# Attention units of two chunks of one batch, two tokens side by side on a partition, and more sums by accumulating DMA

## Chip, cores and metric

One core of a Trainium2 chip. The metric is the device time of one execution in microseconds (us). Each kernel was run beside the kernel before on the same chip, and fast runs are compared with fast runs; a run over 1.5% above the fastest of its kernel doesn't count as fast. A ratio is the mean time of one kernel's fast runs over that of the other's of the same rounds, so it is not quite the ratio of the medians that are quoted.

The engines: PE multiplies matrices (PEld are its weight loads), DVE is VectorE, ACT is ScalarE, POOL is GpSimd, SP is SyncE. In a line of a profile, L303 is line 303 of that kernel.

## The reference

Gated linear attention, token by token, followed by a two-layer block with a rational function in its middle. 4 batches, 8 heads, 768 tokens, head size 48; model width 384, inner width 2048.

```python
f = 1.0 / (1.0 + np.exp(-f_logit))
for t in range(S):
    state = f[:, :, t, :, None] * state + einsum('bhd,bhde->...', k[:, :, t], v[:, :, t])   # outer product k v^T
    y[:, :, t] = einsum('bhd,bhde->bhe', q[:, :, t], state)
x = y as (3072 tokens, 384)
h = x @ w_in
P = a[0] + a[1]*h + a[2]*h**2 + a[3]*h**3
Q = 1.0 + abs(b[0])*abs(h) + abs(b[1])*h**2
out = (P / (Q + 1e-6)) @ w_out
```

(The outer product is written in short here.) A kernel does this by chunks of 128 tokens: what a token gets from earlier chunks goes through the state (`q` times state), and what it gets from its own chunk goes through a masked matrix of scores (`scm`) times `v`. Both are summed into `y`.

## The kernel before

The work is cut into 12 units of 256 tokens. Before the change, a unit is one chunk of 128 tokens of two batches (`j` is the batch). All instructions of all units stand in one fixed list of steps (`STEPS`), which was tuned by hand. A unit has steps for the cumulative sums of the gates (`cs`), transposes (`tp`), scores (`sc`) and the update of the state (`sv`), a step `y`, then `xe` (its copy to `xT`), then two groups of the wide part: `hp = w_in . xT`, its copy, squares and sums, logarithm and exponential, and `op = gall . w_out`.

Loads take one DMA for each tensor and batch, in rows of one head of one token (48 x 4 B = 192 B):

```python
def rows(eng, dst, src, n):
    c, u = units[n]
    for j in range(UB):                                    # UB = 2
        eng.dma_start(out=dst[:, j],
                      in_=src[u * UB + j, :, c * C:(c + 1) * C, :].rearrange("h t d -> t h d"))
```

A head takes 48 columns, so it is put together from pieces of at most 32 output rows (`quad`). `r` says which 32 of the 128 output rows, and so which 32 columns of the PE array, a matmul uses.

```python
def mm(j, p, i, quad, lhsT, rhs):
    lo, hi = cols[p % 2, quad]
    qd = 3 * (p // 2) + quad
    r = 64 * i + 32 * (qd % 2)
    nc.tensor.matmul(y[r:r + hi - lo, qd // 2, j, :], lhsT[:, lo:hi], rhs,
                     start=False, stop=True, skip_group_check=True)

todo = [(j, p, i, quad) for j in range(UB) for half, quad in cols
        for p in range(half, HP, 2) for i in range(2)]
if s["c"] > 0:
    for j, p, i, quad in todo:                             # 32 matmuls of 48 rows x 32 columns
        r = slice(64 * i, 64 * i + D)
        mm(j, p, i, quad, s["st"][r, j, p, :], s["qkT"][r, j, 0, p, :])
for j, p, i, quad in todo:                                 # 32 matmuls of 128 rows x 32 columns
    mm(j, p, i, quad, s["vn"][:, j, p + HP * i, :], s["scm", j][:, i * HP + p, :])
```

So the number of rows used changes once inside a unit. Two sums of the rational function are done in one of several ways, chosen group by group of 24 groups: by DVE, by an accumulating DMA, or (`u` only) by PE through the identity.

```python
P_BY_DMA = {5, 7, 8, 10, 11, 13, 14, 15, 16, 17, 18, 19, 20, 21, 22}
U_BY_DMA = {3, 7, 8, 9, 10, 12, 13, 14, 17, 19, 21, 23}

def m_p(n):
    s = mg[n]
    if n in P_BY_DMA:
        nc.gpsimd.dma_start(out=s["t"], in_=s["pb"], accum_op=ALU.add)
    else:
        nc.vector.tensor_add(s["t"], s["t"], s["pb"])
```

## Time and profile before

| | kernel before |
|---|---|
| time, median (2 runs) | 254.75 us (253.52 to 255.97) |
| busy PE / DVE / ACT, of a span of 252.3 us | 207.8 / 213.6 / 207.6 us |
| all `y` phases together, first clearing to last start | 13.0 us |
| PE at half clock | 27.3 us, all in the first 81.5 us |

The page of the kernel before gives busy times of the engines, and the clock granted to PE in 40 slices of the span (9 is full):

```profile
PE 207.8 (82%) x2423; PEld 142.1 (56%) x2423; DVE 213.6 (85%) x238; ACT 207.6 (82%) x203; POOL 60.4 (24%) x77
...
PEclk9977959795897999999999999999999999999999
```

Three engines are nearly equally full, none above 85%, and the clock is full once the start is over.

### The profile page before, as it was taken

Reading aid. Unit: us, or ns where it says so; the run is one execution under the profiler, and the core shown is the slowest. Engines: PE = TensorE matmul, PEld = TensorE weight load, DVE = VectorE, ACT = ScalarE, POOL = GpSimd, SP = SyncE. Lnnn points to the kernel's source line nnn. Section 1 sums busy time; section 2 is a strip of 40 time slices with the busy share of each in tenths; the row PEclk is TensorE's granted clock in tenths of the full one; section 3 lists DMA queues with packets and bytes.
Section 4 is the critical chain, followed back from the end, with each engine's and each line's share of the span. In section 5 each row is a group of like instructions: output and inputs, shape, how many; then the busy total and the mean of one; then the engine's idle time right before and its main releaser. Section 6 shows DMA issues by size and latency. Waiting matters only on the chain.

```text
span 252.3 us, 5762 instructions
## 1 busy us (share of the span) xinstructions
PE 207.8 (82%) x2423; PEld 142.1 (56%) x2423; DVE 213.6 (85%) x238; ACT 207.6 (82%) x203; POOL 60.4 (24%) x77
## 2 busy tenths in 40 slices
PE   8667366946988898887998969989999999997754
PEld 2234254835664666565766746866576676574432
DVE  7122168899999999999999999979999999999940
ACT  2425427799899999998996999998999899999841
POOL 8046019000510200412223142124115022041100
PEclk9977959795897999999999999999999999999999
DMA  7999989999999996898999999489458859529921
GB/s 122 171 205 166 174 162 109 194 175 195 188 154 177 175 197 128 169 194 100 199 225 197 188 182 196 106 168 166 85 118 181 63 113 188 129 56 214 226 78 62
DMA packets 111338, 39.70 MB, mean 157 GB/s; under 512 B 101201, under 2 KB 107089, under 8 KB 111313
## 3 DMA queue, kind: packets, MB, share of 16 engines
q0 software_dynamic: 31792, 18.88, 54.3%
q1 hardware_dynamic: 79232, 20.45, 43.9%
q8 instruction: 19, 0.31, 0.6%
q14 instruction: 7, 0.05, 0.1%
q10 hardware_dynamic: 288, 0.00, 0.1%
HBM read 25.17 MB, written 4.72 MB: 118 GB/s over the span
## 4 chain that ended last, share of the span: by engine, by line
DVE 27%; DMA 25%; PE 14%; ACT 13%; issue 10%; SPq 9%; POOL 1%; DVEq 0%; POOLq 0%; ACTq 0%
DMA z<-h 9%; DMA t<-pb 8%; SPq L163 7%; PE hp L322 6%; DVE gall L407 5%; DMA qn<-in_q_dram 4%; DVE h L341 4%; PE op L424 4%; ACT y L336 4%; DVE scm L260 4%; DVE qkp L197 3%; DMA fn<-in_f_logit_dram 3%; ACT qi L377 3%; ACT lq L372 2%; DVE t L387 2%
## 5 line engine op out<-in xcount | busy, mean ns | idle before, releaser
L322 PE MATMUL hp<-xT,w_in_sb 128*128 128x256 bf16 x576 | 71.9, 280 | 3.7 <-ACT xT L309 2.1
L424 PE MATMUL op<-w_out_sb,gall 128*128 128x384 bf16 x368 | 67.1, 331 | 6.5 <-ACT osb L212 4.2
L322 PEld LDWEIGHTS <-w_in_sb 128*128 128x128 bf16 x576 | 56.9, 100 | 16.1 <-issue 5.8
L424 PEld LDWEIGHTS <-gall 128*128 128x128 bf16 x384 | 36.3, 98 | 31.3 <-issue 5.9
L336 ACT CAST y<-hp 128x1024 bf16<-128x1024 f32 x48 | 48.3, 1017 | 5.5 <-PE hp L322 4.9
L377 ACT ACTIVATE qi<-lq 128x2048 bf16<-128x2048 f32 x24 | 46.2, 1925 | 0.1
L372 ACT ACTIVATE lq<-z,sig 128x2048 f32<-128x2048 bf16 x18 | 36.2, 2011 | 5.1 <-DMA z<-h 5.0
L260 DVE TENSOR_TENSOR scm<-sc,mask 128x1024 bf16<-128x1024 f32 x24 | 29.1, 1214 | 6.5 <-PE sc L251 6.5
L341 DVE TENSOR_TENSOR h<-y 128x2048 bf16<-128x2048 bf16 x24 | 29.1, 1214 | 1.7 <-DMA z<-h 1.7
L364 POOL DMA_DIRECT2D z<-h x12 | 12.1, 1005 | 76.4 <-ACT A L190 25.4
L407 DVE TENSOR_TENSOR gall<-t,qi 128x2048 bf16<-128x2048 bf16 x24 | 29.0, 1215 | 1.5 <-DMA t<-pb 1.5
L396 POOL DMA_DIRECT2D t<-pb x15 | 14.8, 990 | 61.0 <-DVE t L387 56.1
L387 DVE TENSOR_TENSOR t<-t,h 128x2048 bf16<-128x2048 bf16 x24 | 28.9, 1215 | 0.0
L163 POOL DMA_DIRECT2D vpd<-in_v_dram x24 | 24.8, 1139 | 13.6 <-PE cs L182 13.5
L212 ACT COPY qkT<-tp 128x2048 bf16<-128x2048 bf16 x8 | 15.1, 1884 | 11.6 <-PE tp L206 11.6
L206 PE MATMUL tp<-ident,qkp 128*128 128x128 bf16 x192 | 14.5, 235 | 10.7 <-DVE qkp L197 10.0
L390 DVE TENSOR_SCALAR pb<-y,a_sb 128x2048 bf16<-128x2048 bf16 x24 | 19.3, 805 | 1.8 <-ACT y L336 1.0
L206 PEld LDWEIGHTS <-qkp 128*128 128x128 bf16 x192 | 12.9, 106 | 13.1 <-DVE qkp L197 12.0
L382 DVE TENSOR_SCALAR t<-y,a_sb 128x2048 bf16<-128x2048 bf16 x24 | 19.8, 825 | 0.1
L190 ACT ACTIVATE A<-cs 128x768 f32<-128x768 f32 x24 | 18.5, 818 | 0.6 <-PE cs L182 0.6
L197 DVE TENSOR_TENSOR qkp<-qn,A 128x768 bf16<-128x768 f32 x12 | 11.4, 950 | 8.5 <-DMA qn<-in_q_dram 8.5
L197 DVE TENSOR_TENSOR qkp<-kn,A 128x768 bf16<-128x768 f32 x12 | 11.4, 950 | 7.8 <-DMA kn<-in_k_dram 4.9
(63 smaller groups left out, 232.3 us busy)
## 6 DMA issues: line engine op xcount, KB each, us to landing
t<-pb POOLq DMA_DIRECT2D x15, 512.0 KB, 6.1
z<-h POOLq DMA_DIRECT2D x12, 512.0 KB, 6.1
fn<-in_f_logit_dram SPq DMA_DIRECT2D x24, 192.0 KB, 4.7
kn<-in_k_dram SPq DMA_DIRECT2D x24, 192.0 KB, 5.5
qn<-in_q_dram SPq DMA_DIRECT2D x24, 192.0 KB, 5.8
out_dram<-osb SPq DMA_DIRECT2D x24, 192.0 KB, 3.4
vpd<-in_v_dram POOLq DMA_DIRECT2D x24, 96.0 KB, 7.3
wst<-in_moe_w_in_dram SPq DMA_DIRECT2D x4, 384.0 KB, 8.5
```

The costliest lines, as they stand in the source:

```text
L163: eng.dma_start(out=dst[:, j], in_=src[u * UB + j, :, c * C:(c + 1) * C, :].rearrange("h t d -> t h d"))
L197: nc.vector.tensor_mul(paired(s["qk"][:, i]), s[("qn", "kn")[i]].rearrange(nat, i=2), s["A", i].rearrange(nat, i=2))
L206: nc.tensor.transpose(tp[:, j, i, p, :], s["qk"][:, i, p, j].rearrange("t i d -> t (i d)"), ident)
L260: nc.vector.tensor_mul(m, s["sc", j].rearrange("s i p t -> s (i p) t"), mb)
L322: nc.tensor.matmul(hp[:, e, :], w_in_sb[:, kk, f * P:(f + 1) * P], xT[:, kk, :], start=(kk == 0), stop=(kk == KD - 1))
L336: nc.scalar.copy(part_of(tile_of(n, "y"), half), mg[n]["hp", half].rearrange("p a n -> p (a n)"))
L341: nc.vector.tensor_mul(s["h2"], s["y"], s["y"])
L372: nc.scalar.activation(lq if whole else part_of(lq, half), s["u"] if whole else s["u", half].rearrange("p a n -> p (a n)"), AF.Ln, scale=s ...
L377: nc.scalar.activation(part_of(tile_of(n, "qi"), part, parts), part_of(mg[n]["lq"], part, parts), AF.Exp, scale=-1.0)
L387: nc.vector.tensor_mul(s["t"], s["t"], s["h2"])
L407: nc.vector.tensor_mul(galls[m][:, lo:lo + w, :].rearrange("p a n -> p (a n)"), part_of(s["t"], part, parts), part_of(s["qi"], part, parts))
L424: nc.tensor.matmul(ops[m, b], galls[m][:, mm, b * C:(b + 1) * C], w_out_sb[:, mm, :], start=(mm == 0), stop=(mm == KF - 1))
```

## The change

Its intent, as the diff reads: a unit becomes two successive chunks of one batch, with tokens 2p and 2p+1 side by side on partition p. A row of a load is then two tokens of one head, 384 B, and a load needs one DMA instead of two. Nine more sums become accumulating transfers (27 to 36), which relieves PE and DVE. The start is reordered, and the list of steps was made anew.

The core of the diff (the list of steps, the masks, the cumulative sums, the state update and the start are cut):

```diff
-P_BY_DMA = {5, 7, 8, 10, 11, 13, 14, 15, 16, 17, 18, 19, 20, 21, 22}
+P_BY_DMA = {4, 5, 6, 7, 9, 10, 11, 12, 13, 14, 15, 16, 17, 18, 19, 20, 21, 22}
-U_BY_DMA = {3, 7, 8, 9, 10, 12, 13, 14, 17, 19, 21, 23}
+U_BY_DMA = {2, 3, 4, 5, 6, 7, 8, 9, 11, 13, 15, 16, 17, 18, 19, 20, 21, 22}
...
+    def rows(src, n):
         c, u = units[n]
-        for j in range(UB):
-            eng.dma_start(out=dst[:, j],
-                          in_=src[u * UB + j, :, c * C:(c + 1) * C, :].rearrange("h t d -> t h d"))
+        return src[u, :, c * UB * C:(c + 1) * UB * C, :].rearrange("h (p b) d -> p h (b d)", b=UB)
...
-        cols = {(1, 1): (0, 32), (0, 0): (ZC, ZC + 32), (1, 2): (32, 64), (0, 1): (ZC + 32, 64)}
-
-        def mm(j, p, i, quad, lhsT, rhs):
+        cols = {(1, 1): (-16, 16), (0, 0): (0, 32), (1, 2): (16, 48), (0, 1): (32, 48)}
+
+        def head(p, i, quad):
             lo, hi = cols[p % 2, quad]
             qd = 3 * (p // 2) + quad
...
+            r = slice(64 * i + 32 * (qd % 2), 64 * i + 32 * (qd % 2) + hi - lo)
+            k_ = slice(64 * i, 64 * i + D)
+            for cc in range(UB):                           # the two chunks of the unit
+                w = slice(CH * cc, CH * cc + CH)
+                o = y[r, qd // 2, :, w]
+                if s["c"] + cc > 0:
+                    nc.tensor.matmul(o, s["st"][cc][k_, p * D + lo:p * D + hi], qcols(s, k_, p, w), ...)
+                for b in range(UB):                        # the two tokens of a partition
+                    v0 = (((p + HP * i) * UB + cc) * UB + b) * D
+                    nc.tensor.matmul(o, vf[:, v0 + lo:v0 + hi],
+                                     s["scm", p // 2][:, i, p % 2, b, :]..., ...)
...
+        for odd, quad in cols:
+            for p in range(odd, HP, 2):
+                for i in range(2):
+                    head(p, i, quad)
+            if (odd, quad) == (1, 1):
+                (clear the 16 rows that the pieces at -16 and at 16 have filled with a neighbour's columns)
```

`v` of a unit lies in `vz`, where each chunk fills 64 of 128 partitions and the rest stays zero, so `scm` matmuls keep 128 rows. The order inside `head` is: state (48 rows), `scm`, `scm` (128 rows), and the same for the second chunk. A unit has 96 matmuls for 64, and the number of rows changes 64 times instead of twice, counting the step from the clearing into the first state matmul. (The four first units have no state for their first chunk: 80 matmuls and 32 changes.)

## The prediction

> **What bounds the kernel now.** I read the table by windows first, because a mean over the span mixes three stages. This is the kernel before, cut at 80 and 230 us; the columns after the length are the busy time of PE, PEld, DVE, ACT and POOL, then granted clock, DMA share and GB/s.
>
> ```profile
> 0.00:80.00 80.00, 55.52 (x577) 36.74 (x578) 54.13 (x67) 52.09 (x52) 23.77 (x39) 0.84 1.26 168
> 80.00:230.00 150.00, 138.64 (x1767) 97.78 (x1766) 147.36 (x160) 143.19 (x142) 34.83 (x36) 0.99 0.90 155
> 230.00:252.00 22.00, 13.65 (x80) 7.62 (x79) 12.15 (x13) 12.26 (x11) 1.84 (x2) 1.00 0.59 139
> ```
>
> From 80 to 230 us three engines are nearly full at once: DVE 98% (147.36/150), ACT 95%, PE 92%. DVE ends this stage, but whatever adds more than some 11 us to PE there passes it. In the first 80 us nothing is full except the DMA engines; PE runs on 0.84 of its clock. The chain that ended last says the same of the start: it goes through the DMA queue's issues and through loads.
>
> ```profile
> 13.06 5.91 SPq L163
> 19.02 1.00 SPq L163
> 20.07 1.68 SPq L163
> 21.79 11.02 DMA qn<-in_q_dram
> 32.90 0.97 DVE qkp L197
> ```
>
> So until 33 us unit 1 waits for its q. That is what the wider rows aim at. The third view is PE's own order of time around one attention output `y`, late in the kernel at full clock, and the same early at half clock (start, length, instruction, count):
>
> ```profile
> 180.73 0.19 PE L268 MATMUL y<-zeros 128*128 128x1 bf16 x2
> 180.85 0.63 PE L277 MATMUL y<-qkT,state 48*32 48x128 bf16 x32
> 181.41 0.63 PE L277 MATMUL y<-scm,vpd 128*32 128x128 bf16 x32
> 181.97 1.47 PE L424 MATMUL op<-w_out_sb,gall 128*128 128x384 bf16 x8
> ```
>
> ```profile
> 58.02 1.04 PE L277 MATMUL y<-qkT,state 48*32 48x128 bf16 x32
> 59.00 1.05 PE L277 MATMUL y<-scm,vpd 128*32 128x128 bf16 x32
> ```
>
> One such matmul takes 216 to 219 ns alone, so at 180 us 32 of them start within 0.63 - 0.216 = 0.41 us. The single records show how: four start 3 to 4 ns apart (their results go to four different groups of 32 output rows), and the next four start 56 ns after the first of them. A matmul of 128 columns thus occupies its 32 columns of the array for 56 ns, and four run side by side. From the last state matmul to the first scm matmul (48 rows to 128 rows) it is 146 ns, in 9 of 9 cases after 80 us: 90 more than 56. The same surcharge stands wherever the shape changes: full-width hp to the 48-row sc takes 205 ns where hp to hp takes 109, sc to full-width hp 149 where sc occupies 56. At half clock the state to scm step took 241 ns, a group of four about 107.
>
> **What the Trainium skill says.** (1) TensorEngine Tiling (Array Packing), Tiling Modes, Key Properties: "Changing tiling mode (not just tile) drains the TensorE", and different tiles can run in parallel. The trace agrees on both: 90 to 97 ns for a change, four matmuls per 56 ns. (2) TensorE: Matmul & The Clock Gate, Part 1: the clock goes to half by how busy PE was in windows of about 3.4 us. The trace agrees: its clock records change in multiples of 3413 ns, 27.3 of the first 81.5 us lie at half clock, and none from there to 252 us, where PE is dense. What counts as busy the page does not settle here; see the rivals. (3) DMA: Bandwidth & Descriptors, Why small descriptors are slow: a fixed overhead per packet and descriptor. The DMA records agree: packets of 192 B took 19.1 ns on average, of 1536 B 71.7 ns, so eight times the bytes for 3.8 times the time.
>
> **The change part by part.** Twelve units remain, each of 256 tokens, but of one batch.
>
> Loads: 73,728 packets of 192 B become 36,864 of 384 B. Between the two points above, 384 B come to 19.1 + 192 x (71.7 - 19.1)/1344 = 26.6 ns (estimate). That is 1405 us of engine time down to 981; v (24,576 packets at 29.0 ns, now half as many at perhaps 33) 713 down to 405. Over 16 engines this frees 46 us of one mean engine. Nine more accumulating transfers (27 to 36) cost 9 x 128 packets x 349 ns / 16 = 25 us. So DMA gets lighter, and half as many issues leave the start by perhaps 8 to 10 us sooner: unit 1's q should land near 23 instead of 33 us.
>
> DVE: 3 adds of t and pb and 2 of z and h fewer at 1.215 us, one qkT copy more (1.2), the state product in 20 halves (about 0.3 each) in place of 10 at 0.55, masks and three memsets of v at the start (about 3). Net about -1 us of 213.6. ACT: one qkT copy (1.9) and the split Ln of four groups (2 x 1.115 to 2.01) fewer: about -2.5 us. Neither pays for much.
>
> PE: the `u` sums go from 6 groups to 2: two thirds of 12.4 us, -8.3. `cs` takes four matmuls a unit for two: 24 x 162 ns = +4. `sc` has 32 of 64 columns a unit for 16 of 128, now four side by side in place of two: about 0. `sv`, its late state part and the clearing matmuls: about +4.
>
> `y` is the large part. The program's order shows for each head piece six matmuls in a row into the same 32 output rows: state, scm, scm for the first chunk, then the same for the second. Two things of before are lost. No two neighbours lie in different columns, so each takes its whole 56 ns. And the row shape changes from 48 to 128 and back inside every triple: 146 + 56 + 146 = 348 ns a triple. A unit has 16 pieces x 2 triples: 32 x 348 = 11.1 us, where before it took 0.63 + 0.56 = 1.2. The four first units (no state for their first chunk) have 16 x (56 + 146 + 146 + 56 + 56) = 7.4 us. Sum: 8 x 11.1 + 4 x 7.4 = 118.5 us for 14.4 us before (the busy time of that line): +104.
>
> PE in all: 207.8 - 8.3 + 4 + 4 + 104 = 312 us busy at the clock of before. Nothing hides this: PE alone is then longer than the old span, its order is fixed, and while a y of 11 us runs, ACT and DVE have only what two hp halves have left them, some 5 to 7 us. PE becomes the bound. It still has to wait for the first loads and masks (some 10 us), at the tail for the last sums and products (before: 22 - 13.65 = 8 us), and a few us for ACT after each y. With 20 of idle: 312 + 20 = about 332 us.
>
> The clock can add to it. In y only 3 x 53 of 348 ns stream (46%), on 32 of 128 columns. In the trace before, the window of 40.5 to 43.9 us, with y and long gaps, was followed by half clock, as was the one before 78 us (streaming 39% of it); windows that streamed 56% or more at full clock kept it. At half clock a triple is 241 + 107 + 241 = 589 ns, so after the first 3.4 us (10 triples) the other 22 take 13 us: 16.4 us for a unit instead of 11.1, and the matmuls after it start slow. That is up to 8 x 5.3 + 4 x 3 = 54 us more: about 385 us. I take the two as about equally likely, with part of the y phases sharing a window with dense work, and put the middle nearer the first: 345 us.
>
> **The rivals.** (a) The early loads decide, as the change intends: PE's work stays hidden, the start shrinks by 8 to 10 us, and the time is about 244. For it: DVE is the fullest engine and its order has been fitted to the new times. Against it: DVE loses only 1 us in the stage of 150 us, and PE was at 92% there, with room for 11 us, not for 104. (b) Only the side-by-side running is lost, and the change of row shape inside the same 32 columns costs nothing: y is then 32 x 3 x 56 = 5.4 us, in all +46 us on PE, 254 busy, about 275 us. For it: every change in the trace that I can read stands at the end of a group, where other causes could lie. Against it: the same 90 to 97 ns stands at five kinds of change, and scm follows state directly without a semaphore. (c) The nine more accumulating transfers are late and DVE or ACT wait for them: 6.1 us median landing, hidden behind PE if PE is the bound; a few us at most. (d) The half clock lasts through most of each unit: above 385.
>
> **Range and chances.** (b) gives the region below 290, the main sum without throttling 320 to 340, with it 370 to 395. The range is 288 to 392. Faster by over 2% needs that both PE effects are wrong: 0.07. Within 2% needs a near-balance of the load gain with half of PE's cost: 0.03. Slower: 0.90.
>
> **What would show it.** Right: the y lines busy over 90 us in place of 14.4; in PE's order of time, state and scm alternating with starts of about 146, 56, 146 ns; PE above 90% of the span, DVE and ACT at 60 to 70%; the chain of waits led by PE's y line. The start: unit 1's q landing before 27 us, packets down from 111,338 to about 63,000. The clock row shows whether y runs throttled. Wrong: y starts still 3 to 15 ns apart within a head, or under 40 us busy for y, means that same-column matmuls overlap and my main term fails; then the time falls to 245 to 260. If PE is full but with gaps of 56 ns throughout, rival (b) holds. If PE's busy time is as said but the time is over 390, the fixed order makes PE wait for ACT.

## The result and the profile after

| | before | after |
|---|---|---|
| time, median | 254.75 us (253.52 to 255.97; 2 runs) | 383.85 us (382.33 to 385.36; 2 runs) |
| span of the profiled run | 252.3 | 380.3 |
| busy PE / DVE / ACT | 207.8 / 213.6 / 207.6 | 356.7 / 214.4 / 207.1 |
| all `y` phases together | 13.0 us | 152 us |
| PE at half clock, within the span | 27.3 us | 161.6 us |
| DMA packets | 111,338 | 62,910 |

The ratio of the fast runs is 1.507, with an interval of 1.466 to 1.547. The kernel is correct and half again as slow. From the page of the changed kernel: busy times, granted clock, the chain that ended last by engine and by line, and its two costliest groups (busy us, mean ns of one; the two groups overlap each other, so their sum is more than the `y` phases take):

```profile
PE 356.7 (94%) x3095; PEld 208.1 (55%) x3095; DVE 214.4 (56%) x257; ACT 207.1 (54%) x200; POOL 63.8 (17%) x83
...
PEclk9958869589696695596699589559859956966999
...
PE 81%; DVE 6%; ACT 5%; DMA 4%; issue 3%; POOL 1%; POOLq 0%; DVEq 0%; ACTq 0%
PE y L307 24%; PE y L303 16%; PE op L455 14%; PE hp L353 14%; PE tp L212 3%; DMA vz<-in_v_dram 3%; PE cs L188 2%; ACT y L367 2%; DMA t<-pb 2%; PE sc L264 2%; DVE scm L276 2%; PE sv L246 1%; ACT lq L403 1%; PE u L387 1%; PE op L518 1%
...
L307 PE MATMUL y<-scm,vz 128*32 128x128 bf16 (+1 forms) x768 | 115.0, 273 | 0.0
L303 PE MATMUL y<-qkT,state 48*32 48x128 bf16 (+1 forms) x320 | 83.7, 262 | 0.0
```

DVE and ACT do the same work as before to within 1 us; they only wait more. 40% of the chain is the two `y` lines. PE's order of time shows how they run (start, length, engine, line, operation, tiles, count). At full clock:

```profile
169.61 0.23 PE L303 MATMUL y<-qkT,state 48*32 48x128 bf16 x1
169.76 0.28 PE L307 MATMUL y<-scm,vz 128*32 128x128 bf16 x2
169.98 0.23 PE L303 MATMUL y<-qkT,state 48*32 48x128 bf16 x1
170.14 0.29 PE L307 MATMUL y<-scm,vz 128*32 128x128 bf16 x2
```

and 5 us later in the same `y`, at half clock:

```profile
175.04 0.29 PE L303 MATMUL y<-qkT,state 48*32 48x128 bf16 x1
175.26 0.40 PE L307 MATMUL y<-scm,vz 128*32 128x128 bf16 x2
175.58 0.29 PE L303 MATMUL y<-qkT,state 48*32 48x128 bf16 x1
```

Before, 32 of these started within 0.41 us. Now one triple of state, `scm`, `scm` takes 0.37 us at full clock (steps of 156, 66 and 149 ns in the single records) and 0.54 us at half. A `y` lasts 14.5 to 15.5 us in the eight units with a full state, 6.8 to 8.9 us in the four first ones. Over the middle of the run (length, busy time of PE, PEld, DVE, ACT, POOL, granted clock, DMA share, GB/s), PE is at 99.5%:

```profile
80.00:350.00 270.00, 268.75 (x2295) 156.20 (x2294) 144.93 (x161) 146.39 (x141) 40.25 (x44) 0.77 0.50 97
```

The waits (total, times, longest) show who pays: ACT sits idle 125 us, about ten us a unit, until a `y` is done, and DVE waits where its matmul stands behind `y` in PE's order.

```profile
ACT xT L340 <- PE y L307: 125.4, 12, 14.6
...
DVE scm L276 <- PE sc L264: 26.8, 10, 14.8
```

The start went as the change intends. Idle time of DVE before the product of `q` (last column: us and what ended it), before and after:

```profile
L197 DVE TENSOR_TENSOR qkp<-qn,A 128x768 bf16<-128x768 f32 x12 | 11.4, 950 | 8.5 <-DMA qn<-in_q_dram 8.5
```

```profile
L204 DVE TENSOR_TENSOR qkp<-qn,A 128x768 bf16<-128x768 f32 x12 | 11.4, 950 | 3.8 <-ACT A L197 3.8
```

DVE never waits for `q` any more. The `q` of unit 1 is issued at 7.5 us, and no early load of `q` took over 15.1 us to land, so it was there by 22.7 us at the latest (32.8 before). It did not help: the product of unit 1 starts at 33.2 us (32.9 before), because PE is in the 8.5 us of unit 0's `y` and ACT's factor `A` comes after it.

### The profile page after: what moved, and what is told of

Read it like the earlier page. It is cut to its first block, busy times and chain, and to the rows that moved or that the text cites. A ratio compares the mean times of both kernels' runs of the same rounds, so it can differ in the third digit from the quotient of the medians.

```text
span 380.3 us, 7065 instructions
## 1 busy us (share of the span) xinstructions
PE 356.7 (94%) x3095; PEld 208.1 (55%) x3095; DVE 214.4 (56%) x257; ACT 207.1 (54%) x200; POOL 63.8 (17%) x83
## 2 busy tenths in 40 slices
DMA packets 62910, 44.49 MB, mean 117 GB/s; under 512 B 51616, under 2 KB 57504, under 8 KB 62880
## 4 chain that ended last, share of the span: by engine, by line
PE 81%; DVE 6%; ACT 5%; DMA 4%; issue 3%; POOL 1%; POOLq 0%; DVEq 0%; ACTq 0%
PE y L307 24%; PE y L303 16%; PE op L455 14%; PE hp L353 14%; PE tp L212 3%; DMA vz<-in_v_dram 3%; PE cs L188 2%; ACT y L367 2%; DMA t<-pb 2%; PE sc L264 2%; DVE scm L276 2%; PE sv L246 1%; ACT lq L403 1%; PE u L387 1%; PE op L518 1%
## 5 line engine op out<-in xcount | busy, mean ns | idle before, releaser
L307 PE MATMUL y<-scm,vz 128*32 128x128 bf16 (+1 forms) x768 | 115.0, 273 | 0.0
L303 PE MATMUL y<-qkT,state 48*32 48x128 bf16 (+1 forms) x320 | 83.7, 262 | 0.0
L340 ACT ACTIVATE xT<-y,sig 128x768 bf16<-128x768 f32 x12 | 10.8, 900 | 125.4 <-PE y L307 125.4
L353 PE MATMUL hp<-xT,w_in_sb 128*128 128x256 bf16 x576 | 75.8, 289 | 1.4 <-ACT y L367 1.2
L455 PE MATMUL op<-w_out_sb,gall 128*128 128x384 bf16 x368 | 73.6, 355 | 3.7 <-ACT osb L218 2.0
L303 PEld LDWEIGHTS <-state 48*32 48x32 bf16 (+1 forms) x320 | 29.4, 92 | 51.8 <-issue 40.2
L455 PEld LDWEIGHTS <-gall 128*128 128x128 bf16 x384 | 39.5, 105 | 32.8 <-issue 12.3
L307 PEld LDWEIGHTS <-vz 128*32 128x32 bf16 (+1 forms) x768 | 37.7, 98 | 31.9
L403 ACT ACTIVATE lq<-z,sig 128x2048 f32<-128x2048 bf16 x22 | 44.2, 2011 | 0.1
L334 DVE TENSOR_TENSOR state<-sv,alast 128x192 bf16<-128x192 f32 x20 | 7.0, 352 | 54.9 <-PE sv L253 48.1
L372 DVE TENSOR_TENSOR h<-y 128x2048 bf16<-128x2048 bf16 x24 | 29.1, 1217 | 15.5 <-ACT y L367 15.5
L218 DVE COPY qkT<-tp 128x2048 bf16<-128x2048 bf16 x5 | 6.1, 1224 | 31.8 <-PE tp L212 31.8
L163 POOL DMA_DIRECT2D vz<-in_v_dram x24 | 20.7, 957 | 2.3 <-DVE vz L506 1.9
```

The source lines that it names most:

```text
L163: nc.gpsimd.dma_start(out=vz[n % NV][w, :, cc].rearrange("p h b d -> p h (b d)"), in_=rows(v, n)[w])
L303: nc.tensor.matmul(o, s["st"][cc][k_, p * D + lo:p * D + hi], qcols(s, k_, p, w), start=False, stop=True, skip_group_check=True)
L307: nc.tensor.matmul(o, vf[:, v0 + lo:v0 + hi], s["scm", p // 2][:, i, p % 2, b, :].rearrange("s (b t) -> s b t", b=UB), start=False, stop=T ...
L353: nc.tensor.matmul(hp[:, e, :], w_in_sb[:, kk, f * P:(f + 1) * P], xT[:, kk, :], start=(kk == 0), stop=(kk == KD - 1))
L372: nc.vector.tensor_mul(s["h2"], s["y"], s["y"])
L403: nc.scalar.activation(lq if whole else part_of(lq, half), s["u"] if whole else s["u", half].rearrange("p a n -> p (a n)"), AF.Ln, scale=s ...
```

## The experiments

Two theories of `y` were tied together in the prediction: that neighbours in the same 32 columns run one after another (56 ns each instead of 4), and that a change of row shape costs 90 ns more. The experiments take them apart, then ask what the rest of the change is worth.

### The changed kernel with `y` in another order

Only the order of the 96 matmuls of a unit is changed, with the same operands: in two groups of pieces (the clearing lies between them), all state matmuls, then all `scm` matmuls, with the four pieces of different columns as neighbours. The row shape changes 4 times a unit, counting the clearing, for 64.

```diff
-        for odd, quad in cols:
-            for p in range(odd, HP, 2):
-                for i in range(2):
-                    head(p, i, quad)
+        for group in ([(1, 1)], [(0, 0), (1, 2), (0, 1)]):
+            for odd, quad in group:
+                for cc in range(UB):
+                    for p, i in four(odd):
+                        from_state(p, i, quad, cc)
+            for odd, quad in group:
+                for cc in range(UB):
+                    for b in range(UB):
+                        for p, i in four(odd):
+                            from_v(p, i, quad, cc, b)
```

> The changed kernel with only the order of the y matmuls changed: same matmuls, same operands, same clears, but grouped so that four neighbours go to four different groups of 32 output rows, and all state matmuls of a part stand before all scm ones (4 changes of row shape a unit, not 64). My theory (order of y alone made the loss): y takes 24 x 56 + 4 x 90 ns = 1.7 us a unit in place of 7 to 15, PE busy falls to 210 to 220 us, the time to 240 to 252 us. Rival 1 (the loss is in the new layout, its 1088 smaller matmuls for 704, or the nine more accumulating transfers): y stays over 60 us busy or the time over 300 us.

Measured: 242.74 us (241.07 to 243.44, 4 runs) for 254.12 of before; ratio 0.954, interval 0.947 to 0.961. The order of these matmuls alone makes the difference of 141 us to the changed kernel, and what is left of the change is a gain. Busy times and the chain on its page, and one `y` in PE's order of time:

```profile
PE 207.9 (86%) x3091; PEld 148.6 (62%) x3095; DVE 212.1 (88%) x257; ACT 204.3 (85%) x200; POOL 63.7 (26%) x83
...
DVE 31%; ACT 27%; PE 14%; DMA 12%; issue 11%; POOL 2%; POOLq 0%; DVEq 0%; ACTq 0%
```

```profile
155.37 0.19 PE L289 MATMUL y<-zeros 128*128 128x1 bf16 x2
155.49 0.29 PE L303 MATMUL y<-qkT,state 48*32 48x128 bf16 x8
155.71 0.41 PE L309 MATMUL y<-scm,vz 128*32 128x128 bf16 x16
155.94 0.18 PE L289 MATMUL y<-zeros 128*16 128x1 bf16 x4
156.05 0.52 PE L303 MATMUL y<-qkT,state 48*32 48x128 bf16 x24
156.50 0.57 PE L309 MATMUL y<-scm,vz 128*32 128x128 bf16 x27
157.22 0.49 PE L309 MATMUL y<-scm,vz 128*32 128x128 bf16 x21 [0.16 <-issue]
```

The whole `y`, 102 matmuls with the clearing, takes 1.76 us from the first start to the last in seven of the eight units with a full state. The one shown takes 2.13: between its 27th and 28th `scm` matmul stands a pause that the profile doesn't explain. PE is back at the 208 us of before, DVE leads the chain again.

### The same with neighbours in the same columns

The four shape changes stay, but the matmuls of one piece now follow each other. This is the order in which the prediction has each take its whole 56 ns.

```diff
             for odd, quad in group:
-                for cc in range(UB):
-                    for p, i in four(odd):
+                for p, i in four(odd):
+                    for cc in range(UB):
                         from_state(p, i, quad, cc)
```

(and likewise for `scm`)

> As y_side (4 changes of row shape a unit), but all matmuls of one head piece stay in a row, so that neighbours share their 32 output rows. Separates the two causes in y. If a column group is held 56 ns by each matmul: y is 96 x 56 ns + 0.4 = 5.8 us a unit at full clock, PE busy about 265, time 262 to 285 us. If columns of one group overlapped after all (only the shape changes cost), y stays under 2.5 us a unit and the time is that of y_side. It also tells what the clock counts: y streams over 90% of its time here but on a quarter of the columns; if the clock counts columns it goes to half in y and the time nears 300; if it counts streaming time it stays full.

Measured: 244.5 us in one run. `y` takes 1.87 us, not near 5.8:

```profile
156.83 0.30 PE L303 MATMUL y<-qkT,state 48*32 48x128 bf16 x8
157.06 0.44 PE L309 MATMUL y<-scm,vz 128*32 128x128 bf16 x16
```

The 16 `scm` matmuls, in runs of four for the same columns, start within 0.44 - 0.22 = 0.22 us, in four rounds of four, with mostly 13 to 16 ns between starts and 56 to 67 ns from round to round. One group of columns alone would need 4 x 56 ns for its four. So the starts fit four column groups that work at once, each at its own 56 ns, although the program lists them one group after the other. (The records don't name the columns, so this is read from the times.) That half of my theory of `y` has fallen.

### 16 and 32 changes of shape a unit

Between the 4 of the first experiment and the 64 of the changed kernel. With 16, each of the four kinds of pieces goes state, `scm` for each chunk, four pieces side by side; with 32 this is done for two pieces at a time. The cut draws both edits together:

```diff
+        for odd, quad in cols:
+            for cc in range(UB):                 # 16: for p, i in four(odd) inside
+                for p, i in four(odd):           # 32: "for p in ..." outside of cc, "for i" inside
+                    from_state(p, i, quad, cc)
+                for b in range(UB):
+                    for p, i in four(odd):
+                        from_v(p, i, quad, cc, b)
```

> As y_side with four neighbours side by side, but the row shape changes 16 times a unit rather than 4. If each change costs 90 ns: y 24 x 56 + 16 x 90 = 2.8 us a unit, 1.1 more than y_side, PE busy 12 to 14 us more, time 0 to 12 us above y_side. If changes of shape cost nothing, y_side's y to within 0.2 us a unit.

> As y_side, but the row shape changes 32 times a unit (two neighbours side by side, then the next two). With 150 ns from the last matmul of one shape to the first of the next: 16 x (150 + 56 + 150) = 5.7 us a unit at full clock, 48 us more PE than y_side, PE busy about 256, time 258 to 275 us if the clock stays full. As in the changed kernel some 45% of y's time streams; if that alone brings the clock down within 5.7 us, half of the y phases run slow and the time is 275 to 300 us. If the changes cost nothing: 243 to 247 us.

Measured, 16 changes: 246.54 us in one run, `y` 3.08 us a unit, PE busy 220.0. Single records: state to `scm` 156 ns, `scm` to state 149. PE gains 12.1 us of work and the time 3.8: most of it goes into PE's slack. Measured, 32 changes: 278.71 us in one run (before 254.23), 4 us above the range expected for full clock, `y` 5.98 us, PE busy 252.2. From 80 to 215 us PE is busy for 134.63 of 135 us, so the slack is used up and PE is the bound. The clock row of its page:

```profile
PE 252.2 (91%) x3091; PEld 167.5 (61%) x3095; DVE 213.8 (77%) x257; ACT 205.8 (74%) x200; POOL 63.5 (23%) x83
...
PEclk9985995975999999999999999999999999999999
```

The clock stays full from 69 us on.

### The kernel before, with `scm` directly behind its state matmul

The opposite test: nothing of the change, only the order of `y`.

```diff
-        if s["c"] > 0:
-            for j, p, i, quad in todo:
+        for j, p, i, quad in todo:
+            if s["c"] > 0:
                 mm(j, p, i, quad, s["st"][r, j, p, :], s["qkT"][r, j, 0, p, :])
-        for j, p, i, quad in todo:
             mm(j, p, i, quad, s["vn"][:, j, p + HP * i, :], s["scm", j][:, i * HP + p, :])
```

> The kernel before, with one thing of the change alone: each head piece's scm matmul stands directly behind its state matmul. Nothing else of the change is in it. My theory: 32 pairs x (146 + 146) ns = 9.3 us a unit for ten units (1.2 before), PE busy +80 at full clock, more when the clock falls to half; time 315 to 350 us. Rival 1 (the new layout is to blame): within 3% of 254.75 us.

Measured: 366.98 us in one run, above the expected range; PE is busy for 331.6 us of a span of 365.2. One stretch of its order of time:

```profile
170.85 0.23 PE L277 MATMUL y<-qkT,state 48*32 48x128 bf16 x1
171.01 0.23 PE L277 MATMUL y<-scm,vpd 128*32 128x128 bf16 x1
171.17 0.23 PE L277 MATMUL y<-qkT,state 48*32 48x128 bf16 x1
```

Each step is 157 to 160 ns at full clock and 216 to 217 ns at half; here too the mean granted clock falls to 0.80, which the expectation had named but not counted. With none of the new layout, the order alone costs 113 us.

### The changed kernel's own order, with one row shape

If it is the change of shape and nothing else about alternating, then the order of the changed kernel must be cheap once both kinds of matmul use 128 rows. The state was given a copy for each half of the partitions with the other half zero, so that `q` of both halves is multiplied and one half adds zeros. The order of `y` is untouched. It costs twice as many products of the state on DVE and some clearing at the start.

```diff
-    states = [[consts.tile([P, HP * D], ...
+    states = [[consts.tile([P, 2, HP * D], ...
...
-                    nc.tensor.matmul(o, s["st"][cc][k_, p * D + lo:p * D + hi], qcols(s, k_, p, w),
+                    nc.tensor.matmul(o, s["st"][cc][:, i, p * D + lo:p * D + hi], qcols(s, slice(0, P), p, w),
```

> The changed kernel with its y matmuls in exactly the order of the change (six in a row into the same 32 output rows, state between scm), but every one of 128 rows: the state of each half of the heads lies in a tile whose other half is zero, so the state matmul no longer changes the row shape. Costs 20 more half-height state products on DVE (about 7 us) and a few more small matmuls. If the change of row shape alone makes the loss: y under 3 us a unit, clock full after 80 us, time 243 to 255 us. If neighbours in the same 32 columns matter (the other half of my prediction's y term): y 5 to 6 us a unit, time 265 us or more.

Measured: 250.38 us in one run for 254.3 of before; correct; `y` 2.50 us a unit with the clearing, PE busy 215.4 us, DVE 221.8 (8 to 10 us more than in the other forms of this kernel, and DVE leads its chain with 55%, which fits its being behind the first experiment).

```profile
160.75 0.23 PE L305 MATMUL y<-qkT,state 128*32 128x128 bf16 x1
160.82 0.28 PE L309 MATMUL y<-scm,vz 128*32 128x128 bf16 x2
160.88 0.27 PE L305 MATMUL y<-qkT,state 128*32 128x128 bf16 x2
160.94 0.28 PE L309 MATMUL y<-scm,vz 128*32 128x128 bf16 x3
```

State and `scm` alternate as in the changed kernel, in the same order and into the same columns, and 8 of them start in less time than one triple took. The cause is settled: it is the change between 48 and 128 rows, 64 times a unit.

### What the rest of the change is worth

With `y` out of the way, the change gains 11.4 us (254.12 to 242.74). Where? DVE's busy time is 212.1 us for 213.6, so it is not less work. DVE's idle time fell: 252.3 - 213.6 = 38.7 us before, 240.7 - 212.1 = 28.6 now, and 8.9 of these 10.1 us lie in the first 80, where DVE has done 63.0 us of work (third busy time) for 54.1:

```profile
0.00:80.00 80.00, 60.57 (x916) 42.60 (x919) 62.99 (x91) 56.34 (x58) 22.14 (x38) 0.89 1.10 197
```

(Not all of that is progress: some clearing of tiles and the masks, which I had put at about 3 us, moved to DVE at the start.) Four runs undo or extend one part each, from this kernel, called "reordered" from here on.

Loads of `q`, `k` and `f` again as two DMAs in rows of 192 B:

```diff
-            nc.sync.dma_start(out=at_[n][name].rearrange("p h b d -> p h (b d)"), in_=rows(src, n))
+            for b in range(UB):
+                nc.sync.dma_start(out=at_[n][name][:, :, b, :], in_=rows(src, n)[:, :, b * D:(b + 1) * D])
```

> y_side with q, k and f loaded in two transfers each of 192 B rows as in the kernel before (same bytes, same tiles; v stays as in the change). If the wide rows are what y_side gains by: the first hp of unit 1 and the dense stretch come 6 to 10 us later, time 248 to 255 us. If the gain is from the sums or the new order of steps: within 2 us of y_side's 242.7.

Measured: 246.58 us (243.43 to 249.4, 4 runs); two of the four are over 1.5% above the fastest and don't count as fast. The ratio of the fast runs is 0.962 (0.956 to 0.968) where the wide rows gave 0.954 (0.947 to 0.961): 0.008 x 254 = 2 us, with intervals that overlap. The profiled run (249.4 us) is one of the two slow ones, so its trace is not set against the fast profile of the reordered kernel.

So the rows are worth about 2 us when all goes well, not shown beyond doubt. The four times spread more than those of the reordered kernel (243.4 to 249.4 for 241.1 to 243.4); why is not shown.

The sums shared out as before (27 transfers, `u` of six groups on PE):

```diff
-P_BY_DMA = {4, 5, 6, 7, 9, ..., 22}
+P_BY_DMA = {5, 7, 8, 10, 11, 13, ..., 22}
-U_BY_DMA = {2, 3, 4, 5, 6, 7, 8, 9, 11, 13, 15, ..., 22}
+U_BY_DMA = {3, 7, 8, 9, 10, 12, 13, 14, 17, 19, 21, 23}
 (and the steps of u on PE set directly ahead of their logarithms)
```

> y_side with the sums shared out as in the kernel before: 27 accumulating transfers for 36, six groups of u on PE for two, 15 sums on DVE for 10. If DVE is the bound after the start: 5 x 1.215 = 6 us more, time 246 to 251 us. If the accumulating transfers bring nothing (their landing is waited for in the same places): within 1.5 us of y_side.

Measured: 281.47 us (277.23 to 282.67, two of the four runs slow), ratio 1.111 (1.105 to 1.117), far more than any sum of the parts. ACT waits 19.6 us for `u` on PE, in 10 places: where I put these steps in the fixed list, they come too late. (An earlier placement deadlocked when it was built.) The run says nothing of the sums.

So the same question without PE: nine of the 36 transfers as DVE additions at the same place in the list, 27 transfers left.

```diff
-P_BY_DMA = {4, 5, 6, 7, 9, 10, ..., 22}
+P_BY_DMA = {5, 7, 10, ..., 22}
-U_BY_DMA = {2, 3, 4, 5, 6, 7, 8, 9, 11, 13, 15, ..., 22}
+U_BY_DMA = {2, 3, 5, 7, 8, 9, 11, 13, 17, 19, 21, 22}
```

> y_side with nine of its 36 accumulating transfers done in place by DVE instead (27 left, as many as in the kernel before; order of steps unchanged). Tells what the nine more transfers are worth. If DVE is the bound after the start: 9 x 1.215 = 10.9 us more, time 250 to 254 us. If their landings cost as much as the sums: within 2 us of 242.7.

Measured: 251.03 us (249.91 to 252.71), ratio 0.989 (0.982 to 0.996): 8.3 us slower than the reordered kernel. DVE's busy time rises from 212.1 to 221.9. The first 80 us are as in the reordered kernel (62.74 us of DVE's work), and the loss comes later, where DVE is full:

```profile
80.00:215.00 135.00, 123.67 (x2028) 90.57 (x2029) 134.00 (x149) 124.56 (x124) 28.24 (x32) 1.00 0.75 145
```

The starts of `xT`, the copy behind each `y`, show where the sums count, from ACT's order of time (the last two kernels have one list of steps, the first has another, so only the two compare exactly):

| start of `xT`, us | unit 1 | unit 4 | unit 11 (last) |
|---|---|---|---|
| kernel before | 43.0 | 97.0 | 220.8 |
| reordered | 39.2 | 90.2 | 207.4 |
| reordered, nine sums back on DVE | 38.5 | 90.7 | 215.0 |

Against the kernel before, the reordered one is 6.8 us ahead at unit 4 and 13.4 at the last. With the sums back on DVE the first lead is there, and what is lost is lost after unit 4.

This comparison gives all nine sums to DVE; in the kernel before, four of them were PE's. It therefore says that the transfers are needed: the new layout brings DVE work of its own, and without them DVE would have 221.9 us, more than before.

And four more transfers (40 in all):

> y_side with four more sums given to accumulating transfers (40 for 36; only groups 0, 1 and 23 stay on DVE): DVE 4 x 1.215 = 4.9 us less. If DVE is still the bound and the transfers are hidden: 238 to 241 us, the fastest of all. If the transfers land too late or the DMA engines are full: 242 us or more.

```diff
+ P_BY_DMA: 2, 3, 8 in addition;  U_BY_DMA: 12 in addition
```

Measured: 250.70 us (249.99 to 251.51), ratio 0.988 (0.984 to 0.992): a miss, 8 us worse than with 36 although DVE's busy time falls by 4 us. In its place stand waits for landings (this kernel first, then the one with 36; total, times, longest):

```profile
DVE pb L435 <- DMA t<-pb: 6.2, 3, 4.0
```

```profile
DVE pb L435 <- DMA t<-pb: 1.6, 2, 1.3
```

ACT's wait for `z<-h` rises likewise, from 2.1 to 8.2 us. So these four transfers land too late for their places in the list of steps; whether they would pay at other places was not tried.

### All orders of `y` side by side

| kernel | shape changes a unit | `y` of a unit, us | PE busy, us | time, us |
|---|---|---|---|---|
| new order, different columns as neighbours | 4 | 1.76 | 207.9 | 242.7 |
| new order, same columns as neighbours | 4 | 1.87 | 211.9 | 244.5 |
| 16 changes | 16 | 3.08 | 220.0 | 246.5 |
| 32 changes | 32 | 5.98 | 252.2 | 278.7 |
| the changed kernel | 64 | 14.5 to 15.5 (half clock in it) | 356.7 | 383.9 |
| the changed kernel's order, all 128 rows | none inside | 2.50 | 215.4 | 250.4 |

From 4 to 16 changes each costs (3.08 - 1.76)/12 = 110 ns, from 16 to 32 (5.98 - 3.08)/16 = 181 ns. At 64, all at full clock, `y` would take about 32 x 0.372 = 11.9 us, (11.9 - 5.98)/32 = 185 ns each. What stays the same is the time for one state group with the `scm` behind it, 0.39, 0.38 and 0.37 us (start to start in the single records at full clock) for 16, 32 and 64 changes, although four, two and one matmuls stand side by side in them. So a pair of changes costs about the same however little work stands between, and it pays to put much there. The time follows once PE's slack is used up: with 4 changes PE makes 14% of the chain, with 16 it makes 58% and with 32 it makes 68%. (The second to fourth and the last row are single runs; their times to within 2 or 4 us of the first row say little, their `y` and PE columns come from the traces.)

## Why the prediction was right or wrong

**That it gets slower, and that `y` on PE is the cause: right.** The direction, PE as the new bound, and the chain led by `y` all stand in the profile, and restoring the order of `y` removes the whole loss and 11 us more.

**The surcharge of a shape change: right.** 90 ns over the 56 of a matmul was said; 156 and 149 ns were measured, so 100 and 93. A triple took 372 ns for 348 said; the other 24 ns are these and a gap of 66 for 56.

**"No two neighbours lie in different columns, so each takes its whole 56 ns": wrong.** In the same program order by columns, but with few changes of shape, a matmul starts every 13 to 16 ns (second experiment), which fits four column groups at 56 ns each working at once. It is the shape change that keeps those for other columns from starting early: between two changes here stand just one or two matmuls, all for the same columns in a unit with a full state, and there one sees 66 ns. The sum came out nearly right because in this kernel both always occur together; to that extent it was luck. It also means that rival (b), side-by-side running lost without a cost of shape, has no such size: the run built that way took 244.5 us and not 275.

**The clock: the mechanism right, its weight wrong.** I held full clock and half clock in `y` about equally likely and put the middle nearer full clock: 345. In fact every `y` of a unit fell to half, 3 to 6 us after its start in the units with a full state, and stayed there 2 to 5 us after its end: 161.6 us at half clock. The throttled sum, 385, is what happened (383.85), inside the range of 288 to 392. The terms of it: `y` of a unit 16.4 said and 14.5 to 15.5 measured, since the triple at half clock is 540 ns and not 589; the four first units 10.3 said (7.4 and the 3 for half clock) and 6.8 to 8.9 measured. In the sum, PE's busy time rose by 356.7 - 207.8 = 149 us: 139 are `y` (152 - 13), and 10 are `hp` (75.8 for 71.9) and `op` (73.6 for 67.1) run at half clock behind it. That the rest of PE's parts cancel is borne out by the first experiment: there `u` is 8.4 us less, `cs` 4.9 and `sv` 3.6 more. Idle time of PE: 20 said, 380.3 - 356.7 = 23.6 measured. How much of the time the clock makes is only worked out: with all triples at 372 ns, eight `y` of 11.9 us, and four of some 6.1 (16 pieces at the 0.378 us that they take at full clock) come to 120 us for 152, and with the 10 us of `hp` and `op` that is some 42 us, for the 54 of the prediction. No run holds the clock up with the same order. That the sum of 385 comes so near is in part luck: `y` grew by 139 us for the 158 (104 + 54) said, while the 10 us of `hp` and `op`, 3.6 us more of idle time and the 2 us between the span and the time were not in it.

**Loads: right, but hidden.** Packets 62,910 for about 63,000; a packet of 384 B took 26.7 ns for an estimate of 26.6; `q` of unit 1 landed by 22.7 for "near 23". (The packets of `v` took 36.8 ns for 33.) None of it shows in the time, since unit 1 then waits for PE and ACT.

**DVE and ACT: right that they hardly matter, less so on shares.** Changes of -1 and -2.5 us were said, +0.8 and -0.5 measured. Shares of 60 to 70% were said, 56 and 54% measured, because the span is longer than the middle of the prediction.

**Rival (a) described what lies under `y`.** It said 244, with a start 8 to 10 us shorter; the change with `y` reordered takes 242.7, with 8.9 us less idle time of DVE in the first 80 us. "Neither pays for much", of DVE's and ACT's work, held as well: DVE has 1.5 us less to do. What I had not seen is that the nine transfers have to be there to keep it so (8.3 us). Rival (c), late transfers, stayed hidden in the changed kernel: `t<-pb` is 2% of its chain. It shows up only where PE is not the bound, in the run with 40 transfers.

**What stays open.** Why the clock falls. A matmul of 256 columns lasts 53 ns longer than one of 128 (272 for 219), so I count 53 ns of streaming for 128 columns. In windows of 3.4 us that lie inside a `y` PE then streams 42 to 44% of the time in the changed kernel (47% in the one from 92.4 us) and falls to half clock after each. With 32 changes, where most such windows stream 45% (the one from 96.7 us, for example), the clock stays full. So the share of time alone doesn't decide it. The two differ in how many columns are used at once (32 against 64) and in matmuls per us; no run separates these. And of the shorter start, the share of the wide rows, of half as many issues and of the new order of the first steps was not told apart: the run with narrow rows scatters too much. Nor is it separated whether the number of rows itself matters or only the group of rows that it falls into: 48 against 128 is the one pair that was run.

## What to carry to other kernels

Where small matmuls of different row counts (here 48 and 128) share the array, write all of one row count, then all of the other; for the columns the order made little difference (1.87 us a unit for 1.76). If they must alternate, pad the smaller with zeros to the same number of rows: here 64 changes a unit cost some 13 us, half clock included, and padded matmuls in the very same order 0.7 us (2.50 for 1.76) and some work of DVE. A change that loses much may hide a gain: the new layout was 4.6% faster once the order of one inner loop was mended.

## What the Trainium skill lacked or had wrong

- TensorEngine Tiling (Array Packing), Key Properties, says that changing the tiling mode drains the TensorE, without a size. Here a change between 48 and 128 rows in the same 32 columns made a step of 149 to 160 ns (216 to 245 at half clock), where matmuls of one shape in the same columns stand 56 to 67 ns apart. In all, a change made a `y` longer by 110 ns (few changes) to 185 ns (many). In the kernel before, the same step stands where the rows stay 128 and the columns go from a 32-column group to the full width: 151 to 152 ns from the last `y` matmul to the first `op` in five of six cases.
- TensorE: Matmul & The Clock Gate, Part 3 (Packing small matmuls), has matmuls start and end strictly in program order, "strict FIFO, no reordering". The starts recorded here do not bear that out for matmuls in different columns: in the changed kernel a 16-column clearing matmul started at 172.374 us, ahead of an `scm` matmul that the program has before it, at 172.433. The 16 starts within 0.22 us of the second experiment fit this. PE's ends are modelled in the trace, so only the starts are told.
- The same page, Part 1, does not settle what counts as busy for the clock. Windows inside a `y` that streamed 42 to 44% of the time on 32 columns fell to half clock, windows that streamed 45% on 64 columns kept full clock.
- DMA: Bandwidth & Descriptors gives no time for a packet of the sizes of rows here: 19.1 ns for 192 B and 26.7 ns for 384 B on one engine, both on the queue of SP. The size alone does not set it: the 192 B packets of `v`, on the queue of POOL, took 36.8 ns.
